# A two-stage Fourier and mixer kernel: the set-up of batch 0 and its hand-over to the chunks put in another order

## The chip, the cores and the metric

The kernel runs on one core of a Trainium2 chip. A core has five engines that each work through their own list of instructions in order: TensorE (PE: matrix products; PEld is its weight load), VectorE (DVE), ScalarE (ACT), GpSimd (POOL) and SyncE (SP, which here only issues transfers). GpSimd and ScalarE issue transfers too. An instruction that waits for another engine's result holds up all that stands behind it on its own engine. The metric is the device time of one execution in microseconds.

## The reference, cut to what matters

```python
x: (8, 3136, 256)   U: (3136, 32)   V: (32, 3136)   w1: (256, 1024)   w2: (1024, 256)
X = fft(fft(x, axis=1), axis=2).real          # per batch: 3136 x 256
h = (X.transpose(0, 2, 1) @ U @ V).transpose(0, 2, 1)
u = X + h                                     # rank-32 mixing along the sequence
out = u + relu(u @ w1) @ w2                   # per row, 256 -> 1024 -> 256
```

## The kernel before, in words

**Tables.** The transform along the sequence is done as matrix products with tables of sines (`tabs[0]`) and cosines (`tabs[1]`) that the kernel makes at the start. A table has eight rows i of two halves each, 393 columns wide, and behind these 32 columns that hold U, already transformed. Rows with even i are made whole (`odd_row`); of the rows 7, 5, 3, 1 only the upper half is computed (`phase` on VectorE, a Sin on ScalarE, line 226), and `mirror_even` (line 325) writes the lower half as a mirrored copy, over `turned_copy` (line 318): on GpSimd when the sign is plus (rows 5 and 1 of the sines), on ScalarE when it is minus. The cosine rows are copies of sine rows (`cosine_odd`, `cosine_low`, `cosine_high`) or made by Abs and Sin (lines 232 and 233).

**Input of batch 0.** x of one batch arrives in two halves a = 0, 1, forward (`xf`) and reversed (`xr`). `along_d` (line 360, VectorE) folds the 256 channels into 128 sums and 128 differences (`EOF_`, `EOR_`), `alone` (line 366, GpSimd) copies the lone channel. For batch 0 one half of the fold along the sequence is done on TensorE, as products with an identity or a flip matrix (`fold_pe`, line 756), and evicted to `G` by ScalarE (`evict_g`); the other half on VectorE (`mirror`, `half`, lines 369 and 373). `load_second(a)` loads batch 1's half a into the same `xf` and `xr`; it issues one plain and one indirect transfer from GpSimd's queue and two small ones from SP's. `g_zeros` and `va_zeros` clear the unused parts of `G` and `VA` on GpSimd.

**U.** `transform_u(typ)` gives four steps for the sine table (`us`) and four for the cosine table (`uc`): `contract` (16 products, line 286), `keep` (a copy on ScalarE, line 292), `turn` (8 products, line 299), `evict` (two copies on ScalarE into the table's last 32 columns, lines 304 and 305).

**Sequence products.** `seq(b, par, typ, pn)` (line 411) multiplies `G` with a table, four products each. The call with pn = 0 leaves a copy `ev` on ScalarE, the call with pn = 1 gives on VectorE: a 32-column sum into `TAB` (line 433), an "up" sum (440) and a "down" sum (444) into `A` (typ 1) or `B` (typ 0). The wide result covers 128 channels; the lone channel, one row, is done by `narrow` (line 488), called by `first_channel` for batches 0 and 1 and by `column_steps` for the six others together: 16 products of 32 columns, one copy `evc`, and in `sums(par)` a sum into the row of `VA` (509), a 32-element sum `tc` (515) and, with par = 1, the sum of both `tc` (517). `finish` casts it into `low` (556).

**Hand-over.** `lowrank(0)` (line 599) multiplies `low` and `TAB` to give the low-rank operand `TA`. `chan` (line 562) makes from `A` and `B` the transformed rows `S` (h = 0, copied by ScalarE) and `T` (h = 1, for batch 0 copied by VectorE), in pieces of columns cut at 0, 393, 512, 785, 1177, 1569. `front(c)` (line 627) forms `u` of chunk c, 512 rows: a product of `TA` and `VA` (634), to which VectorE adds `S` and `T` (642), then a transposing transfer on SP's queue (645).

**Chunks.** There are 49 chunks. Each has eight steps j; in a step, `first_product` (two products of 512 columns, line 654, and a Relu on ScalarE, 656), on odd j `second_product` of the chunk before (eight products of 256 columns, line 670, three sums on VectorE, 676 to 679, and the store), then what the dictionary `due` holds for step 8c + j, and at j = 3 the `front` of the next chunk. `spread` puts the fold of batch 1 into steps 4 to 23 and its transform behind that; `column_loads` go to SP's queue from step 8.

**What sets the order.** Up to the end of chunk 0 the order is the one written (`tc.manual_schedule()`, closed at c = 1); after that a planner orders the instructions, except those that `pin` holds. Semaphores between the engines are put in by the framework, from the tiles and the address ranges that two instructions touch. Tiles of one tag share their buffers, so a new one waits until an old one is released: three PSUM buffers for tag "dft", three for "p1", two for "p2", two SBUF buffers for "ev".

Of the kernel before, what the change touches and what calls it, by code (L numbers as in the profile page):

```python
# [27 lines left out]
def kernel(  # L28
# [296 lines left out]
    def mirror_even(t, i):  # L325

        odd_m = (i + 1) // 2 % 2 == 1
        turned_copy(cells(t, i, 0, 1, NH - 1, 1), cells(t, i, NQ - 1, -1, NH - 1, 0),
                    1 if odd_m == (t == 0) else -1)

# [156 lines left out]

    def narrow(nb, stationary, dst, tc_, tag=("dft", 3), late=None):

        t = {}  # L490

        def products():
            pt = t["pt"] = psum.tile([P, QW], FP32, tag=tag[0], name="ptc", bufs=tag[1])
            for n in range(NI // 2):
                for g in range(4):
                    pn, par = divmod(g, 2)
                    i = ktiles(pn)[n]
                    nc.tensor.matmul(pt[g * R:(g + 1) * R], stationary(par, i),
                                     tabs[1][:kp(i), i, par, :],
                                     start=(n == 0), stop=(n == NI // 2 - 1))  # L500
            t["ev"] = wp.tile([P, QW], FP32, tag="ev", name="evc", bufs=2)
            nc.scalar.copy(t["ev"][2 * R:], t["pt"][:2 * R])
        yield products

        def sums(par):
            e, o = (t[k][(2 + par) * R:(2 + par) * R + nb] for k in ("ev", "pt"))
            up = dst[:, HALF // 2 - par:(0 if par else None):-2]
            dn = dst[:, HALF // 2 + 2 - par:HALF + 1 - par:2]
            nc.vector.tensor_tensor(up, o[:, par:NQ], e[:, par:NQ], op=AL.add)
            down = lambda: nc.vector.tensor_tensor(dn, e[:, 1:NQ], o[:, 1:NQ], op=AL.subtract)  # L510
            if late is None:
                down()
            else:
                late.append(down)
            nc.vector.tensor_tensor(tc_[:, par], o[:, NQ:QW], e[:, NQ:QW], op=AL.add)
            if par:
                nc.vector.tensor_tensor(tc_[:, 0], tc_[:, 0], tc_[:, 1], op=AL.add)
        for par in range(2):
            yield lambda par=par: sums(par)

    def column_steps():
# [18 lines left out]
        yield fold_c  # L540
        yield from narrow(NB, lambda par, i: GC[par][:kp(i), i * NB:i * NB + R], rows, tc_)

# [7 lines left out]
    def first_channel(b, **kw):  # L550
        tc_ = cpool.tile([1, 2, R], FP32, name=f"tc{b}", tag=f"tc{b}")
        dst = VA[b][R:R + 1]
        yield from narrow(1, lambda par, i: G[b][par][:kp(i), i, 256:256 + R], dst, tc_, **kw)

        def finish():
            nc.vector.tensor_copy(low[:1, b * R:(b + 1) * R], tc_[:, 0])
        yield finish
        mid = (HALF + S) // 2
        for lo, hi in ((HALF + 1, mid), (mid, S)):
            yield lambda lo=lo, hi=hi: nc.scalar.copy(dst[:, lo:hi], dst[:, S - lo:S - hi:-1])  # L560

    def chan(b, lo, hi, h, tag=("dft", 3)):
        d = ST[b]
# [4 lines left out]
                         start=False, stop=True)  # L568
        (nc.vector.tensor_copy if b == 0 and h == 1 else nc.scalar.copy)(
            d["ST"[h]][:, lo:hi], pt[:, :hi - lo])  # L570
# [27 lines left out]

    def lowrank(b):
        pt = psum.tile([P, 256], FP32, tag="dft", name="ptt", bufs=3)  # L600
        nc.tensor.matmul(pt[:], low[:, b * R:b * R + P], ones[:], start=True, stop=False)
        for n in range(4):
# [134 lines left out]
    mirror_even(0, 1)  # L737
    alone(0, xr, EOR_)
    alone(0, xf, EOF_)
    g_zeros(0)  # L740
    cosine_odd(4)
# [35 lines left out]
    for part in range(2):  # L777
        along_d(0, xf, EOF_, part)
    fold_pe(0, EOF_)

    def load_second(a):
        load_r(1, a)
        load_f(1, a)
        load_0(1, a, nc.sync)

    load_second(0)
    halve(1)
    mirror(0, slice(0, 128), AL.subtract)
    us[0]()
    us[1]()  # L790
    us[2]()
    busy(3, tabs[0])
# [21 lines left out]
    for par in range(2):  # L814
        half(0, par, slice(256, 258))
    load_second(1)
    evict_g(0)
# [3 lines left out]

    ta_rows(0)
    va_zeros(0)
    nc.gpsimd.memset(TAB[:, 4 * R:].bitcast(I32), 0)
# [10 lines left out]
    narrow_0 = list(first_channel(0, tag=("p2", 2), late=late))  # L835
    seq(0, 0, 0, 0)
    seq(0, 0, 0, 1)
    narrow_0[0]()
    seq(0, 1, 0, 0)
    for step in narrow_0[1:4]:  # L840
        step()
    late.insert(0, seq(0, 1, 0, 1))
    lowrank(0)
    cuts = (0, 393, 512, 785, 1177, HALF + 1)
    for n in range(2):
        for h in range(2):
            chan(0, cuts[n], cuts[n + 1], h, ("p2", 2) if n and h else ("p1", 3))
    tc.no_sync_barrier()
# [3 lines left out]
    for h in range(2):  # L852
        chan(0, cuts[2], cuts[3], h)
    for step in late:
# [7 lines left out]

    due = {n: [lambda n=n: chan(0, cuts[3 + n // 2], cuts[4 + n // 2], n % 2)] for n in range(4)}
    due.update({4: [lambda: last_row(0)], 5: narrow_0[4:5], 6: narrow_0[5:6], 44: [column_flips]})

# [61 lines left out]
```

## Time and profile before

| | us |
|---|---|
| median of 3 runs | 461.48 |
| lowest and highest | 458.42, 462.24 |
| the profiled execution | 462.04 |
| its span, first to last instruction | 459.0 |
| TensorE busy in the span | 443.2 (97%) |
| VectorE, ScalarE, GpSimd busy | 355.9, 296.2, 70.0 |
| mean granted TensorE clock | 0.996 |

Times in rows of the profile are counted from the start of the span. A row of the order of time has start, length, engine, line, operation, out<-in, shapes, the number of instructions, and in brackets the idle time before it with what ended it. Shares of busy time hide that the set-up (the first 40 us or so) and the chunks have different limits. Ends of TensorE's products are modelled, and spans on GpSimd are rough.

### The profile page before, as it was taken

What the parts mean: (1) busy time and instruction counts of PE and PEld (TensorE: products, weight loads), DVE (VectorE), ACT (ScalarE), POOL (GpSimd) and SP (SyncE); (2) the same over time, 40 slices, a digit from 0 to 9 for tenths busy, and PEclk for the clock granted to TensorE, in tenths of its full rate; (3) what the DMA queues carried; (4) which work ended last, traced back from release to release, by engine and by line L of the source; (5) the groups of instructions that cost most, each with busy time, mean ns of one, the idle gap of its engine ahead of it and who ended that gap; (6) DMA issues with size and microseconds to landing.
All of it is one profiled execution on the core that took longest, in us unless ns stands there. A gap on an engine that the chain in (4) does not pass through costs nothing.

```text
span 459.0 us, 8105 instructions
## 1 busy us (share of the span) xinstructions
PE 443.2 (97%) x2989; PEld 323.1 (70%) x3042; DVE 355.9 (78%) x818; ACT 296.2 (65%) x568; POOL 70.0 (15%) x112
## 2 busy tenths in 40 slices
PE   8878999999999999999999999999999999999996
PEld 6435766676777777777777777777777777777775
DVE  8997999878898769976997779967898666443433
ACT  7766645866965577665865577655865586655562
POOL 7980612100022002100102002200000000000000
PEclk9998999999999999999999999999999999999999
DMA  7995888995377826684298436792253323333343
GB/s 212 205 236 103 175 202 159 140 210 147 117 202 185 175 71 163 192 222 121 71 226 205 134 87 178 198 224 76 70 95 113 93 83 102 93 115 96 113 119 110
DMA packets 102955, 66.98 MB, mean 146 GB/s; under 512 B 73526, under 2 KB 99328, under 8 KB 99776
## 3 DMA queue, kind: packets, MB, share of 16 engines
q1 hardware_dynamic: 97762, 40.73, 38.6%
q0 software_dynamic: 5136, 25.74, 20.6%
q8 instruction: 23, 0.38, 0.3%
q14 instruction: 16, 0.13, 0.1%
q10 hardware_dynamic: 18, 0.00, 0.0%
HBM read 29.33 MB, written 25.69 MB: 120 GB/s over the span
## 4 chain that ended last, share of the span: by engine, by line
PE 83%; DVE 8%; issue 2%; DMA 2%; ACT 2%; POOL 1%; SPq 1%; DVEq 0%; POOLq 0%
PE p L670 34%; PE p L654 31%; PE pt L426 5%; PE ph L634 4%; PE pth L402 2%; DVE eor L360 2%; DVE eof L360 2%; DMA ut<-u 1%; PE pst L577 1%; PE pst L586 1%; DVE u L642 1%; DMA cr<-in_x_dram 1%; SPq L482 1%; PE ptt L603 1%; PE pg L761 1%
## 5 line engine op out<-in xcount | busy, mean ns | idle before, releaser
L656 ACT ACTIVATE h<-p 128x512 bf16<-128x512 f32 x392 | 223.6, 598 | 129.9 <-PE p L654 106.0
L654 PE MATMUL p<-u,w 128*128 128x512 bf16 x733 | 209.8, 379 | 2.6 <-ACT h L656 0.9
L670 PE MATMUL p<-w,h 128*128 128x256 bf16 x1568 | 204.0, 273 | 1.3
L670 PEld LDWEIGHTS <-h 128*128 128x128 bf16 x1568 | 153.1, 98 | 51.8 <-issue 0.6
L654 PEld LDWEIGHTS <-w 128*128 128x128 bf16 x784 | 106.0, 144 | 36.2 <-issue 3.0
L676 DVE TENSOR_TENSOR o<-p,ut 128x4 f32<-128x4 f32 (+1 forms) x100 | 16.5, 165 | 58.2 <-PE p L670 55.3
L55 POOL DMA_INDIRECT xf<-in_x_dram,xidx x16 | 20.3, 1269 | 184.7 <-DVE eof L360 172.6
L679 DVE TENSOR_TENSOR o<-p,ut 128x254 f32<-128x254 f32 (+1 forms) x100 | 40.9, 409 | 0.0
L678 DVE TENSOR_TENSOR o<-p,ut 128x254 f32<-128x254 f32 (+1 forms) x100 | 40.9, 409 | 0.0
L360 DVE TENSOR_TENSOR eor<-xr 99x1024 bf16<-99x1024 f32 x32 | 39.7, 1250 | 0.0
L360 DVE TENSOR_TENSOR eof<-xf 99x1024 bf16<-99x1024 f32 x32 | 39.0, 1236 | 0.0
L642 DVE TENSOR_TENSOR u<-ph,S 128x512 bf16<-128x512 f32 (+15 forms) x64 | 35.2, 559 | 0.0
L642 DVE TENSOR_TENSOR u<-ph,T 128x512 bf16<-128x512 f32 (+15 forms) x64 | 35.1, 559 | 0.0
L634 PE MATMUL ph<-va,ta 128*128 128x512 bf16 (+15 forms) x126 | 29.3, 329 | 0.1
L426 PEld LDWEIGHTS <-g 98*128 98x128 bf16 (+1 forms) x152 | 14.8, 98 | 13.6 <-issue 1.1
L369 DVE TENSOR_TENSOR eos<-eof,eor 99x1024 bf16<-99x1024 bf16 (+2 forms) x32 | 20.4, 654 | 0.0
L373 DVE TENSOR_TENSOR g<-eos 99x2048 bf16<-99x2048 bf16 (+3 forms) x18 | 18.6, 1048 | 0.2
L588 DVE TENSOR_TENSOR S<-evd,pst 128x392 bf16<-128x392 f32 (+1 forms) x24 | 13.6, 566 | 6.5 <-PE pst L586 6.1
L433 DVE TENSOR_TENSOR tab<-pt,ev 128x32 bf16<-128x32 f32 x32 | 6.1, 190 | 15.4 <-PE pt L426 14.3
L426 PE MATMUL pt<-tabs,g 98*128 98x425 bf16 x80 | 17.4, 344 | 0.0
L426 PE MATMUL pt<-tabc,g 98*128 98x425 bf16 x72 | 15.5, 343 | 0.6 <-ACT tabc L304 0.6
L73 POOL DMA_DIRECT2D xr<-in_x_dram x14 | 8.1, 575 | 40.5 <-DVE eor L360 40.2
(170 smaller groups left out, 361.6 us busy)
## 6 DMA issues: line engine op xcount, KB each, us to landing
out_dram<-o SPq DMA_DIRECT2D x48, 512.0 KB
xr<-in_x_dram POOLq DMA_DIRECT2D x14, 784.0 KB, 6.7
xr<-in_x_dram SPq DMA_DIRECT2D x2, 784.0 KB
ut<-u SPq DMA_TRANSPOSE x49
w<-in_moe_w_ch_dram POOLq DMA_DIRECT2D x1, 512.0 KB, 14.8
out_dram<-o SPq DMA_DIRECT2D x4, 128.0 KB
va<-in_moe_V_dram POOLq DMA_DIRECT2D x2, 196.0 KB, 5.0
xf<-in_x_dram,xidx POOLq DMA_INDIRECT x16, 7.3
```

What stands on the lines that cost most here:

```text
L55: nc.gpsimd.indirect_dma_start(out_, None, bass.AP(t.tensor, t.offset, [[w, rows], [1, w]]), bass.IndirectOffsetOnAxis(idx, 0), element_of ...
L360: pin(nc.vector.tensor_tensor(dst[:, a, :, part * P:(part + 1) * P].rearrange("p i (k t) -> p i k t", k=2), lo, hi, op=AL.subtract if part ...
L369: pin(nc.vector.tensor_tensor(EOS[:, a, :, cols], EOF_[:, a, :, cols], EOR_[:, a, ::-1][:, :, cols], op=op))
L373: pin(nc.vector.tensor_tensor(G[b % 2][par][:, :, cols], EOS[:, 0, :, cols], EOS[:, 1, :, cols], op=AL.add if par == 0 else AL.subtract))
L426: nc.tensor.matmul(pt[:], g[:kp(i), i, P * typ:P * (typ + 1)], tabs[typ][:kp(i), i, par, :], start=(n == 0), stop=(n == NI // 2 - 1))
L634: nc.tensor.matmul(ph[:, col:col + hi - lo], TA[b % 2][:k, s * P:(s + 1) * P], VA[b % 2][:k, lo:hi], start=True, stop=True)
L642: nc.vector.tensor_tensor(u[:, s, col:col + hi - lo], ph[:, col:col + hi - lo], src, op=AL.add)
L654: nc.tensor.matmul(p1[:], W1[:, s, j::JT], k["u"][:, s, :], start=(s == 0), stop=(s == 1))
L656: LAST[0] = nc.scalar.activation(k["h"][:, j, :], p1[:], AF.Relu)
L670: nc.tensor.matmul(p2[:, t % w, :], h[:, j, rs], W2[:, j, :], start=(j == 0), stop=(j == JT - 1))
L678: nc.vector.tensor_tensor(o[:, ts, 1:P], p2[:, :w, 1:P], ut[:, ts, 1:P], op=AL.add)
L679: nc.vector.tensor_tensor(o[:, ts, P + 1:D], p2[:, :w, P + 1:D], ut[:, tT, P - 1:0:-1], op=AL.add)
```

## The change

In the set-up of batch 0: the mirrored half of row 1 is a ScalarE copy instead of a GpSimd copy. The two `alone` copies of half 0 and `g_zeros(0)` go to places behind U's first steps in the written order; the identity products of half 0's forward part go behind U's first contraction; `load_second(1)` goes behind `ta_rows(0)`.

In `narrow`: each `tc` sum goes ahead of the row's sum, and the sum of both is written to a place that the caller names: for `first_channel` straight into `low` (`finish` with its cast goes), for `column_steps` into `tc` as before.

In the hand-over: the narrow products of batch 0 and their sums stand ahead of the four sine sequence calls; `lowrank(0)` issues eight products of `ones` into its PSUM tile first; the T copy of columns 393 to 512 is ScalarE's instead of VectorE's; batch 1's T copies are ScalarE's in both. The two pieces of columns 785 to 1177 go from steps 0 and 1 to steps 1 and 2, those of 1177 to 1569 from steps 2 and 3 to 8 and 9 (chunk 1), `last_row(0)` from 4 to 10, and the two ScalarE copies that complete the narrow row from 5 and 6 to 12 and 14.

```diff
     def mirror_even(t, i):
 
         odd_m = (i + 1) // 2 % 2 == 1
-        turned_copy(cells(t, i, 0, 1, NH - 1, 1), cells(t, i, NQ - 1, -1, NH - 1, 0),
-                    1 if odd_m == (t == 0) else -1)
+        dst, src = cells(t, i, 0, 1, NH - 1, 1), cells(t, i, NQ - 1, -1, NH - 1, 0)
+        if i == 1:
+            nc.scalar.copy(dst, src)
+        else:
+            turned_copy(dst, src, 1 if odd_m == (t == 0) else -1)
...
             up = dst[:, HALF // 2 - par:(0 if par else None):-2]
             dn = dst[:, HALF // 2 + 2 - par:HALF + 1 - par:2]
+            nc.vector.tensor_tensor(tc_[:, par], o[:, NQ:QW], e[:, NQ:QW], op=AL.add)
+            if par:
+                nc.vector.tensor_tensor(total, tc_[:, 0], tc_[:, 1], op=AL.add)
             nc.vector.tensor_tensor(up, o[:, par:NQ], e[:, par:NQ], op=AL.add)
...
-            nc.vector.tensor_tensor(tc_[:, par], o[:, NQ:QW], e[:, NQ:QW], op=AL.add)
-            if par:
-                nc.vector.tensor_tensor(tc_[:, 0], tc_[:, 0], tc_[:, 1], op=AL.add)
...
-        yield from narrow(1, lambda par, i: G[b][par][:kp(i), i, 256:256 + R], dst, tc_, **kw)
-
-        def finish():
-            nc.vector.tensor_copy(low[:1, b * R:(b + 1) * R], tc_[:, 0])
-        yield finish
+        yield from narrow(1, lambda par, i: G[b][par][:kp(i), i, 256:256 + R], dst, tc_,
+                          low[:1, b * R:(b + 1) * R], **kw)
...
-        (nc.vector.tensor_copy if b == 0 and h == 1 else nc.scalar.copy)(
+        (nc.vector.tensor_copy if dve else nc.scalar.copy)(
...
-    def lowrank(b):
+    def lowrank(b, fill=0):
         pt = psum.tile([P, 256], FP32, tag="dft", name="ptt", bufs=3)
+        for _ in range(fill):
+            nc.tensor.matmul(pt[:], ones[:, :P], ones[:], start=True, stop=True)
...
     cosine_low(1)
     mirror_even(0, 1)
-    alone(0, xr, EOR_)
-    alone(0, xf, EOF_)
-    g_zeros(0)
     cosine_odd(4)
     load_v()
...
-    fold_pe(0, EOF_)
...
+    alone(0, xr, EOR_)
+    alone(0, xf, EOF_)
     load_second(0)
+    g_zeros(0)
     halve(1)
     mirror(0, slice(0, 128), AL.subtract)
     us[0]()
     us[1]()
+    fold_pe(0, EOF_)
     us[2]()
...
-    load_second(1)
...
     ta_rows(0)
+    load_second(1)
     va_zeros(0)
...
     narrow_0 = list(first_channel(0, tag=("p2", 2), late=late))
-    seq(0, 0, 0, 0)
-    seq(0, 0, 0, 1)
-    narrow_0[0]()
-    seq(0, 1, 0, 0)
-    for step in narrow_0[1:4]:
+    for step in narrow_0[:3]:
         step()
-    late.insert(0, seq(0, 1, 0, 1))
-    lowrank(0)
+    for par in range(2):
+        for pn in range(2):
+            late.append(seq(0, par, 0, pn))
+    late = [late[-1]] + late[:2]
+    lowrank(0, 8)
     cuts = (0, 393, 512, 785, 1177, HALF + 1)
     for n in range(2):
         for h in range(2):
-            chan(0, cuts[n], cuts[n + 1], h, ("p2", 2) if n and h else ("p1", 3))
+            chan(0, cuts[n], cuts[n + 1], h, ("p2", 2) if n and h else ("p1", 3), h > n)
...
     for h in range(2):
-        chan(0, cuts[2], cuts[3], h)
+        chan(0, cuts[2], cuts[3], h, dve=h == 1)
...
-    due = {n: [lambda n=n: chan(0, cuts[3 + n // 2], cuts[4 + n // 2], n % 2)] for n in range(4)}
-    due.update({4: [lambda: last_row(0)], 5: narrow_0[4:5], 6: narrow_0[5:6], 44: [column_flips]})
+    def piece(n, h):
+        return [lambda: chan(0, cuts[n], cuts[n + 1], h, dve=h == 1)]
+
+    due = {1: piece(3, 0), 2: piece(3, 1), 8: piece(4, 0), 9: piece(4, 1), 10: [lambda: last_row(0)],
+           12: narrow_0[3:4], 14: narrow_0[4:5], 44: [column_flips]}
```

More of the change, by code (lines that the diff above doesn't have):

```diff
@@ L486, in column_loads, with narrow @@
                     yield load
-    def narrow(nb, stationary, dst, tc_, tag=("dft", 3), late=None):
+    def narrow(nb, stationary, dst, tc_, total, tag=("dft", 3), late=None):
         t = {}
@@ L540, in column_steps @@
         yield fold_c
-        yield from narrow(NB, lambda par, i: GC[par][:kp(i), i * NB:i * NB + R], rows, tc_)
+        yield from narrow(NB, lambda par, i: GC[par][:kp(i), i * NB:i * NB + R], rows, tc_,
+                          tc_[:, 0])
         def finish():
@@ L560, in first_channel, with chan @@
             yield lambda lo=lo, hi=hi: nc.scalar.copy(dst[:, lo:hi], dst[:, S - lo:S - hi:-1])
-    def chan(b, lo, hi, h, tag=("dft", 3)):
+    def chan(b, lo, hi, h, tag=("dft", 3), dve=False):
         d = ST[b]
```

## The prediction

> **What bounds the kernel now.** I read the page first, then the set-up in order of time, because the diff touches only what is issued before chunk 2, and last the stretches behind it, to see whether a lead survives there. The page's busy shares and slices:
>
> ```profile
> PE 443.2 (97%) x2989; PEld 323.1 (70%) x3042; DVE 355.9 (78%) x818; ACT 296.2 (65%) x568; POOL 70.0 (15%) x112
> ...
> PE   8878999999999999999999999999999999999996
> ...
> PEclk9998999999999999999999999999999999999999
> ```
>
> TensorE is 97% busy. Its gaps lie in the first four slices (11.5 us each), and so does the one dip of the granted clock. So the change can win or lose only in the first 46 us; the sum asks how much earlier the chunks start.
>
> The set-up in order of time (start, length, engine, line, operation):
>
> ```profile
> 10.66 0.53 ACT L323 ACTIVATE tabs<-tabs 99x392 bf16<-99x392 bf16 x1
> 13.21 0.60 ACT L232 ACTIVATE ab<-phe,c 99x394 f32<-99x394 int32 x1
> 14.68 1.51 POOL L321 COPY tabc<-tabs 99x394 bf16<-99x394 bf16 x1
> 14.93 0.58 ACT L773 CAST gu<-pf 99x512 bf16<-99x512 f32 x1
> 15.15 1.16 PE L166 MATMUL idle<-tabs 98*128 98x393 bf16 x6
> 16.25 1.38 POOL L321 COPY tabs<-tabs 99x392 bf16<-99x392 bf16 x1
> 17.19 0.67 DVE L310 TENSOR_SCALAR tabc<-tabc,hv 99x786 bf16<-99x786 bf16 x1
> 17.29 0.62 ACT L233 ACTIVATE tabc<-ab,c 99x394 bf16<-99x394 f32 x1
> 18.28 0.85 PE L286 MATMUL pu<-tabs,gu 98*32 98x393 bf16 x16
> 19.19 0.49 ACT L292 CAST wu<-pu 128x393 bf16<-128x393 f32 x1 [1.27 <-PE pu L286]
> 19.73 0.92 PE L299 MATMUL put<-sel,wu 128*98 128x64 bf16 x8 [0.59 <-ACT wu L292]
> 22.84 1.34 POOL L55 DMA_INDIRECT xf<-in_x_dram,xidx  x1 [0.30 <-issue]
> ```
>
> The chain runs from U's contraction (18.28) over its copy on ScalarE (19.19) and the turning product (19.73) to the same again for the cosine table, and then to the sequence products:
>
> ```profile
> 26.86 0.17 DVE L373 TENSOR_TENSOR g<-eos 99x16 bf16<-99x16 bf16 x1
> 28.04 1.60 PE L426 MATMUL pt<-tabs,g 98*128 98x425 bf16 x8
> 29.09 0.75 POOL L183 MEMSET va<- 1x785 int32 x1
> 29.58 0.91 PE L498 MATMUL ptc<-tabc,g 98*32 98x425 bf16 x16
> 29.86 0.59 DVE L440 TENSOR_TENSOR B<-pt,ev 128x393 bf16<-128x393 f32 x1
> 30.35 0.58 DVE L444 TENSOR_TENSOR B<-pt,ev 128x392 bf16<-128x392 f32 x1
> 30.42 1.62 PE L426 MATMUL pt<-tabs,g 98*128 98x425 bf16 x8
> 30.54 0.51 ACT L502 COPY evc<-ptc 64x425 f32<-64x425 f32 x1 [1.06 <-PE ptc L498]
> 31.15 0.58 DVE L509 TENSOR_TENSOR va<-ptc,evc 1x393 bf16<-1x393 f32 x1 [0.21 <-POOL mc L833]
> 31.39 0.52 ACT L430 COPY ev<-pt 128x425 f32<-128x425 f32 x1 [0.35 <-PE pt L426]
> 32.76 0.18 DVE L517 TENSOR_TENSOR tc<-tc 1x32 f32<-1x32 f32 x1
> 33.04 1.44 DVE L556 CAST low<-tc 1x32 bf16<-1x32 f32 x1
> 33.05 1.40 POOL L182 MEMSET va<- 32x1568 int32 x1
> 34.51 0.19 DVE L433 TENSOR_TENSOR tab<-pt,ev 128x32 bf16<-128x32 f32 x1
> 34.54 0.40 PE L601 MATMUL ptt<-ones,low 128*128 128x256 bf16 x1 [2.50 <-DVE low L556]
> ```
>
> TensorE stands 2.50 us for a cast of 32 elements that takes 1.44 us, as long as the GpSimd memset beside it, and the last `tab` sum queues behind that cast. What the gap does to the clock (busy time of PE, PEld, DVE, ACT, POOL in each microsecond, then the granted clock), and how the first `u` follows:
>
> ```profile
> 34.00:35.00 1.00, 0.46 (x3) 0.28 (x4) 0.97 (x3) 0.00 (x0) 0.95 (x2) 0.51 0.97 164
> 35.00:36.00 1.00, 1.00 (x6) 0.63 (x5) 0.19 (x1) 0.11 (x1) 0.60 (x3) 0.50 0.76 123
> 37.00:38.00 1.00, 1.00 (x9) 0.73 (x8) 0.85 (x3) 0.26 (x1) 0.00 (x0) 0.79 0.57 139
> ...
> 37.15 0.76 DVE L569 CAST T<-pst 128x393 bf16<-128x393 f32 x2 [1.95 <-PE pst L567]
> 38.45 0.68 DVE L642 TENSOR_TENSOR u<-ph,T 128x512 bf16<-128x512 f32 x1
> 42.69 0.57 DVE L569 CAST T<-pst 128x392 bf16<-128x392 f32 x1 [0.86 <-PE pst L567]
> ```
>
> The clock is at half from the end of the gap until about 37.4, some 3 us. Behind that:
>
> ```profile
> 47.00:55.00 8.00, 7.81 (x54) 5.71 (x54) 8.00 (x13) 5.59 (x12) 4.57 (x6) 1.00 0.66 159
> 55.00:63.00 8.00, 7.38 (x50) 5.10 (x48) 8.00 (x16) 3.98 (x8) 4.51 (x5) 1.00 1.10 233
> ...
> 61.38 0.44 PE L654 MATMUL p<-u,w 128*128 128x512 bf16 x1 [0.35 <-DVE u L642]
> ```
>
> From 47 to 63 us VectorE never stops and TensorE waits for its `u`. So the lead that lasts is VectorE's.
>
> **The change, part by part.** Times are on the clock of the profile before.
>
> *1. Mirror of sine row 1 from GpSimd to ScalarE.* GpSimd loses 1.38 us. ScalarE gets 0.53 us (the like copy at 10.66), ahead of the operation at 13.21. In the built program this copy waits for GpSimd's copy out of the same row, which ends at 14.68 + 1.51 = 16.19. ScalarE takes its instructions in order, so it stands from 13.3 to 16.2 and copies until 16.8. Queued behind it is everything from 13.21 to the end of the 17.29 row, 4.70 us, which now ends at 21.5. The `gu` copy moves from 15.51 to 19.1; U's contraction needs it, and starts at 19.1 (before 18.28). The copy at 19.19 now starts at 21.5 and the turning product at 22.0: **+2.3 us** for TensorE and all that follows on it. The ends: if the wait were already met, ScalarE would carry only 0.53 us more, the 19.19 copy would start at 18.45, and this would be -0.7; if nothing overlapped it would be 2.9 + 0.53 = +3.4. I take +2.3, since the rows give both ends of the wait.
>
> That contraction now stands ahead of the identity products (`fold_pe`), which slide into TensorE's new gap between 20.0 and 22.0: nothing, instead of the 0.7 above. VectorE's halving (17.19) waits for the same ScalarE queue and moves by 1.4; its last fold (26.86 + 0.17) then ends by 28.5, ahead of the narrow products at 28.04 + 2.3 = 30.3: nothing.
>
> GpSimd's moves: `alone` and the zeros of G go behind the loads of batch 1, half 0, one of which (22.84) ends at 24.2 in the old order and earlier in the new, with 1.38 us less before it. The G evictions that now wait for those zeros run after 25. The loads of half 1 go ahead of the zeros of VA: these ended at 29.84, the loads wait for a VectorE row that is up to 1.4 late, so 31.3; the first narrow row is written at about 31.9. Cover 0.6 us; without it, up to 1 us. SP issues the same list in the same order.
>
> *2. The clock in the new gap.* TensorE has nothing between 15.15 + 1.16 = 16.3 and 19.1: 2.8 us. The gap of 2.50 us ended at half clock for about 3 us. Then the contraction takes 1.7 for 0.85, and four products of 512 columns take 1.7, for 256 columns take 0.109 at full clock:
>
> ```profile
> 107.34 0.87 PE p L670 x8
> ```
>
> They end at 19.1 + 1.7 + 1.7 = 22.5 and the turning product waits 0.5: **+0.5**. Ends: 0, and +3.0 if all products up to the sequence products run at half clock. [...]
>
> *3. Narrow products first, `low` written by the last sum.* Leaving out the shift of 1 and 2, the narrow products take the slot at 28.04, end at 28.95, and `evc` is there at 29.5. On VectorE: two `tc` sums, the sum into `low` (0.18 each, from 32.76) and two `va` sums (0.58), 1.8 with gaps, to 31.3; a `tab` sum and two B sums (29.86 and 30.35 show 0.5 from start to start), to 32.5. The last `ev` copy has to wait for the buffer which the second B sum frees: 0.52, to 33.1. The last `tab` ends at 33.3 (before 34.70). TensorE has finished at 28.04 + 0.91 + 1.60 + 1.62 = 32.2; the eight filling products need a PSUM buffer that the same B sum frees, and run 8 x 0.109 from 32.5 to 33.4. So the low-rank product starts at 33.4, not 34.54: **-1.1**. Ends: -2.4 (TensorE alone) and 0.
>
> [...]
>
> *4. Warm clock.* The gap of TensorE shrinks to about 0.3. From 34.54 it has five products of 256 columns and 2048 columns of `chan`, 1.4 us at 0.109 per 256, twice that at half clock: at most -1.4. ScalarE's copies in between do not shorten, so I take -1.0, and -0.2 for the 119-column T copy that leaves VectorE ahead of `u` (the pair at 37.15 takes 0.76, one wide copy 0.57): **-1.2**. Ends 0 and -1.6.
>
> *5. Late pieces to chunk 1.* VectorE's wait of 0.86 us for the piece at 42.69 falls away: **-0.86**. The piece's copy and `last_row` are done some 3 us later by the same busy VectorE and are not saved. ScalarE's copies of the narrow row follow into 47 to 55, where it has 2.4 us to spare. Ends 0 and -0.86. Past chunk 1 a planner sets the order: batch 1 loses one VectorE copy, about 0, within 0.4 either way.
>
> Sum: 2.3 + 0.5 - 1.1 - 1.2 - 0.86 = -0.4 us. The profiled execution took 462.04 (span 459.0 and 3.0 around it), 0.56 above the median 461.48, so 461.6 there and **461.1** as a median.
>
> **The rivals.**
> A. *The wait in 1 is met early.* Part 1 gives -0.7 and 2 nothing: -0.7 - 1.1 - 1.2 - 0.86 = -3.9, 457.6. For it: GpSimd's recorded spans are rough. Against: its copies stand there back to back, the next one starts at 16.25.
> B. *Slower: the clock stays low.* The 2.8 us gap at 16.3 keeps the clock at half until the sequence products, +3.0 for +0.5: +2.1, 463.6. It is slower than before as soon as part 2 costs over 0.9. For it: gaps in the products go on after 19.1. Against: at 34.5 three busy microseconds were enough.
> C. *It doesn't do what it says.* The new wait stays, TensorE's later gap still halves the clock, and VectorE finds another wait in chunk 0: 4 and 5 give nothing, 2.3 + 0.5 - 1.1 = +1.7, 463.2. Against: the fills stand right in that gap.
>
> **How the numbers follow.** Forecast 0.62, with 459.8 to 462.6 from the halves of its bounds; A 0.14; B 0.14; C 0.10. The range reaches from A to beyond B and C with part 3 short by 1.1: 457.5 to 464.8. One per cent, about what a measurement of this kernel can tell from no change, is 4.6 us. Below 456.9 lies only more than A: 0.07. Above 466.1 lies B with the later gains missing as well: 0.09. Within: 0.84.
>
> **What would show it.** Part 1: ScalarE idle from 13.3 to 16.2, released by GpSimd, and the turning product at about 22. Part 2: clock near 0.5 between 19 and 22.5. Part 3: a `low` sum of 0.2 us, the fills running until the last `tab`. Part 4: clock 1.0 from there to the first `u`, which ends near 39.6 (before 39.13). Part 5: no wait of VectorE before the second `u`, and the first `o` about 0.4 earlier than before. The forecast is wrong if ScalarE does not stand, or if the clock falls for longer than 3 us.

## The result, and the profile after

| | before | after |
|---|---|---|
| median of 20 executions | 461.80 us | 464.81 us |
| lowest, highest | 458.42, 467.85 | 461.06, 470.49 |
| first profiled execution | 462.04 | 461.43 |

The ratio after to before is 1.0064 [1.0039, 1.0088]: 3.0 us slower, 3.7 us above the forecast of 461.1 and just past the end of the range (464.8). Yet the profiled execution is 0.61 us faster than that of before, where the working had -0.4. Both are true, because the executions of the changed kernel fall into two groups by the mean clock that each lists: five at 0.992 to 0.993 with a median of 461.43, and fifteen at 0.985 or less with one of 465.11. The first profile is of the first kind; a second profile, taken in the experiments, is of the second. Some executions also lose time in a wait of TensorE between 100 and 105 us, far behind the change (4.16 us in one profile, whose row stands under "Both gaps filled", 3.52 us in another). A ratio is taken over the executions within 1.5% of the fastest of their kernel, so it leaves out part of the long ones.

The first profile after, page (span and slices):

```profile
span 459.7 us, 8169 instructions
...
PEclk9889999999999999999999999999999999999999
```

Before, the dip of the clock lay in the fourth slice; now it lies in the second and third. The same execution in order of time; for comparison, first the first `u` and the first `o` of before:

```profile
37.84 0.69 DVE L642 TENSOR_TENSOR u<-ph,S 128x512 bf16<-128x512 f32 x1
50.82 0.16 DVE L676 TENSOR_TENSOR o<-p,ut 128x4 f32<-128x4 f32 x1
```

```profile
14.68 0.52 POOL L321 COPY tabc<-tabs 99x394 bf16<-99x394 bf16 x1
...
15.23 0.52 ACT L330 COPY tabs<-tabs 99x392 bf16<-99x392 bf16 x1 [1.94 <-POOL tabc L321]
18.02 0.97 PE L286 MATMUL pu<-tabs,gu 98*32 98x393 bf16 x16 [1.72 <-ACT gu L773]
...
20.81 0.94 PE L299 MATMUL put<-sel,wu 128*98 128x64 bf16 x8
24.38 1.36 PE L286 MATMUL pu<-tabc,gu 98*32 98x393 bf16 x16
33.61 0.18 DVE L514 TENSOR_TENSOR low<-tc 1x32 bf16<-1x32 f32 x1
35.63 1.05 PE L603 MATMUL ptt<-ones 128*128 128x256 bf16 x8 [0.70 <-DVE B L447]
36.51 0.27 PE L604 MATMUL ptt<-ones,low 128*128 128x256 bf16 x1
38.41 0.69 DVE L645 TENSOR_TENSOR u<-ph,S 128x512 bf16<-128x512 f32 x1
39.02 0.68 DVE L645 TENSOR_TENSOR u<-ph,T 128x512 bf16<-128x512 f32 x1
...
50.42 0.17 DVE L679 TENSOR_TENSOR o<-p,ut 128x4 f32<-128x4 f32 x1
```

ScalarE stands for GpSimd's copy, as forecast, and TensorE stands 1.72 us for ScalarE's `gu`; the turning product comes at 20.81 and the second contraction at 24.38 (before 19.73 and 21.96). The copy into `low` is gone, the fills run until the low-rank product, the first `u` ends at 39.70 (before 39.13), and the first `o` starts 0.40 earlier than at 50.82.

The clock of this execution, by stretches set to the edges of its dip (columns as in the prediction's windows: busy time of PE, PEld, DVE, ACT, POOL, then the granted clock):

```profile
11.81:15.22 3.41, 3.38 (x17) 2.23 (x16) 2.63 (x5) 1.46 (x3) 3.35 (x4) 1.00 1.03 250
15.22:18.63 3.41, 1.70 (x23) 0.74 (x21) 3.38 (x4) 3.33 (x7) 3.41 (x6) 1.00 1.01 214
18.63:22.05 3.42, 3.42 (x22) 1.70 (x15) 3.39 (x6) 3.36 (x8) 2.99 (x5) 0.50 1.08 202
22.05:25.46 3.41, 3.41 (x23) 1.28 (x20) 3.27 (x5) 0.75 (x2) 2.35 (x7) 0.50 1.05 237
```

Half clock for 6.8 us, behind a stretch in which TensorE was busy 1.70 of 3.41 us. A mean clock of 0.992 says the same for the whole span: 2 x 0.008 x 459.7 = 7.4 us at half. By that sum the 0.985 of most executions is 13.9 us. The sum doesn't say where in the span the dips lie.

### The profile page after: what moved, and what is told of

It is laid out like the page before. It is cut to its first block, busy times and chain, and to the rows that moved or that the text cites. A ratio compares the mean times of both kernels' runs of the same rounds, so it can differ in the third digit from the quotient of the medians.

```text
span 459.7 us, 8169 instructions
## 1 busy us (share of the span) xinstructions
PE 447.6 (97%) x3050; PEld 323.5 (70%) x3050; DVE 353.2 (77%) x815; ACT 296.4 (64%) x570; POOL 65.9 (14%) x111
## 4 chain that ended last, share of the span: by engine, by line
PE 88%; DVE 5%; ACT 3%; POOL 1%; issue 1%; DVEq 0%; ACTq 0%; POOLq 0%
PE p L673 35%; PE p L657 34%; PE pt L429 5%; PE ph L637 4%; PE pth L405 2%; PE pg L761 1%; ACT h L659 1%; PE pst L587 1%; PE pst L578 1%; PE ptt L606 1%; DVE eor L363 1%; DVE u L645 1%; DVE va L515 1%; POOL xf L55 1%; DVE eof L363 0%
## 5 line engine op out<-in xcount | busy, mean ns | idle before, releaser
L657 PE MATMUL p<-u,w 128*128 128x512 bf16 x784 | 219.0, 379 | 0.8 <-DVE u L645 0.7
L637 PE MATMUL ph<-va,ta 128*128 128x512 bf16 (+19 forms) x128 | 29.6, 329 | 0.0
```

The costliest lines, as they stand in the source:

```text
L637: nc.tensor.matmul(ph[:, col:col + hi - lo], TA[b % 2][:k, s * P:(s + 1) * P], VA[b % 2][:k, lo:hi], start=True, stop=True)
L657: nc.tensor.matmul(p1[:], W1[:, s, j::JT], k["u"][:, s, :], start=(s == 0), stop=(s == 1))
```

## The experiments

Theory after the result: ScalarE's wait opens the gap on TensorE (part 1), the gap puts TensorE at half clock, for 6.8 us in some executions and for twice that in most (part 2, with rival B's size), and the later parts give what they should. Rivals: the moved narrow products, the fills or the late pieces cost the 3 us; or the slow executions lose their time in the chunks. Executions with a mean clock under 0.99 and the medians, for all kernels run (the later batches' 77 executions of before; for the first 20 no clock is listed). An execution at 0.99 or more is called undisturbed below:

| kernel | executions | of them under 0.99 | median | median of the others |
|---|---|---|---|---|
| before | 77 | 32 | 462.04 | 461.03 |
| after | 20 | 15 | 464.81 | 461.43 |
| before, with the mirror on ScalarE | 12 | 10 | 465.95 | 461.85 |
| after, mirror on GpSimd again | 6 | 0 | 458.52 | 458.52 |
| after, first gap filled | 12 | 2 | 458.92 | 458.51 |
| after, mirror issued first (two batches) | 10 | 4 | 458.50 | 457.90 |
| ... without low-rank fills | 6 | 1 | 458.02 | 457.84 |
| ... late pieces in chunk 0 | 10 | 4 | 463.50 | 459.86 |
| ... with the cast | 4 | 1 | 459.89 | 458.24 |
| ... both gaps filled (two batches) | 16 | 0 | 457.87 | 457.87 |
| before, low-rank gap filled | 10 | 2 | 459.68 | 459.42 |
| before, both gaps filled (two batches) | 16 | 0 | 459.96 | 459.96 |
| after, both gaps filled | 12 | 0 | 460.56 | 460.56 |

### The mirror back on GpSimd

```diff
-        if i == 1:
-            nc.scalar.copy(dst, src)
-        else:
-            turned_copy(dst, src, 1 if odd_m == (t == 0) else -1)
+        turned_copy(dst, src, 1 if odd_m == (t == 0) else -1)
```

> The changed kernel with the mirror of sine row 1 back on GpSimd, all else as changed. Theory (the wait of ScalarE opens a gap of TensorE at 16.3 us, and in most executions the clock stays at half for about 14 us after it, not the 7 of the profiled one): no wait and no long gap, clock 0.996 or more, and the later gains of 3.2 us stay, 458 to 459.5 us, 0.6% under the kernel before. Rival (the later parts, the pieces in chunk 1 and the eight filling products, cost the 3 us): no faster than the changed kernel, 464 to 465.

Ratio to before 0.9899 [0.985, 0.9948], clock 1.0. In order of time:

```profile
15.26 1.38 POOL L321 COPY tabs<-tabs 99x392 bf16<-99x392 bf16 x1
16.70 0.85 PE L286 MATMUL pu<-tabs,gu 98*32 98x393 bf16 x16 [0.39 <-POOL tabs L321]
...
35.76 0.69 DVE L642 TENSOR_TENSOR u<-ph,S 128x512 bf16<-128x512 f32 x1
```

The gap ahead of the contraction shrinks from 1.72 to 0.39 us, and the first `u` starts at 35.76, 2.08 ahead of before's 37.84. So all the other parts together gain, and the 3 us come in only with the mirror on ScalarE. The time is in the 458 to 459.5 expected.

### That edit alone, in the kernel before

```diff
     def mirror_even(t, i):
...
-        turned_copy(cells(t, i, 0, 1, NH - 1, 1), cells(t, i, NQ - 1, -1, NH - 1, 0),
-                    1 if odd_m == (t == 0) else -1)
+        dst, src = cells(t, i, 0, 1, NH - 1, 1), cells(t, i, NQ - 1, -1, NH - 1, 0)
+        if i == 1:
+            nc.scalar.copy(dst, src)
+        else:
+            turned_copy(dst, src, 1 if odd_m == (t == 0) else -1)
```

> The kernel before with that one edit of the mirror alone. Theory: it waits as the changed kernel does, the clock falls at 18 us and once more in the old gap at 32 to 34.5 us, clock 0.985 or less, 465 to 469 us. Rival: within 1 us of the kernel before.

Ratio 1.005 [1.0012, 1.0089]; ten of twelve executions have a clock under 0.99. The profiled one, in stretches as above:

```profile
14.79:18.20 3.41, 1.53 (x9) 0.77 (x8) 1.94 (x2) 2.90 (x6) 2.49 (x6) 1.00 0.95 219
18.20:35.27 17.07, 15.37 (x76) 6.88 (x76) 10.43 (x19) 9.04 (x21) 10.42 (x17) 0.50 0.99 219
```

Half clock for 17.07 us. The edit alone makes the kernel slower. Taken by themselves the other parts gave -2.3 us (458.52 against 460.85, the median of the undisturbed executions of before in that batch); with the long dip there they give only 1.2 (from 466.32 here to 465.11 in the changed kernel, executions under 0.99). In the profiles with a long dip (here and in the changed kernel below) the low-rank stage behind it runs at a clock of 1.0, so that the second dip which was expected here is missing, and there is none for the fills to save; that this makes the difference was not tested. But the row ahead of TensorE's gap here is not ScalarE's:

```profile
16.26 2.36 DVE L363 TENSOR_TENSOR eof<-xf 99x1024 bf16<-99x1024 f32 x2 [1.81 <-DMA xf<-in_x_dram,xidx]
18.68 1.86 PE L764 MATMUL pg<-eof,flip 99*99 99x512 bf16 x4 [2.36 <-DVE eof L363]
```

In this order the column products stand ahead of U's contraction, and they wait for VectorE, which waits for the columns from memory, 1.81 us late here. There is a second cause of a gap at the same place, and it differs from execution to execution. The later runs take it up.

### The gap filled, the wait left in

```diff
-    busy(6, tabs[0])
+    busy(17, tabs[0])
```

> The changed kernel with 17 products without use instead of 6 ahead of U's contraction, so that TensorE is busy from 15.2 to 18.1 us; the wait of ScalarE stays. Theory: clock 0.995 or more, the wait itself costs only the 1.1 us by which U's copy comes later (20.3 for 19.2), 459.5 to 460.5 us. If the wait costs by itself and not through the clock: 464 to 465 with a clock near 1.

Ratio 0.9918 [0.988, 0.9955]; two of twelve executions under 0.99. The profiled one (465.83 us, 0.991) has a clock of 1.0 in the whole set-up; its dip of 6.8 us starts at 104.5, behind a wait of TensorE of 3.52 us. In order of time:

```profile
15.15 3.00 PE L166 MATMUL idle<-tabs 98*128 98x393 bf16 x17
18.08 0.85 PE L286 MATMUL pu<-tabs,gu 98*32 98x393 bf16 x16
...
36.59 0.69 DVE L645 TENSOR_TENSOR u<-ph,S 128x512 bf16<-128x512 f32 x1
```

ScalarE's rows are late as before, U's contraction starts at the same time as in the changed kernel (18.02), and nothing is computed sooner; only the clock stays at 1.0. The first `u` starts at 36.59 for 38.41: 1.82 us is the price of the 6.8 us at half clock, and 36.59 - 35.76 = 0.83 us that of the wait itself (1.1 was expected, and 459.5 to 460.5 us in all).

### The mirror issued ahead of GpSimd's copy

```diff
-    cosine_low(1)
     mirror_even(0, 1)
+    cosine_low(1)
```

> The changed kernel with the calls for the mirror of row 1 and the cosine copy of row 1 exchanged: the mirror stays on ScalarE and waits for nothing on GpSimd. Theory: U's copy starts near 18.5 instead of 20.3, no gap over 1 us, 457 to 458.5 us, faster than both. Rival: 464 to 465.

> The changed kernel with the row-1 sine mirror issued ahead of GpSimd's cosine copy, a second time, for its share of executions with the clock at half on the same chip as the kernel with both gaps filled. Theory: 458.2 us in executions with the clock at 1.0, and 463 or more with a clock of 0.985 in about a quarter (6 of the 22 executions of this head so far).

First batch: ratio 0.9887 [0.9824, 0.995]; second: 0.9941 [0.9885, 0.9996]. In order of time (first batch):

```profile
13.33 0.52 ACT L330 COPY tabs<-tabs 99x392 bf16<-99x392 bf16 x1
16.24 0.85 PE L286 MATMUL pu<-tabs,gu 98*32 98x393 bf16 x16
35.63 0.69 DVE L645 TENSOR_TENSOR u<-ph,S 128x512 bf16<-128x512 f32 x1
```

ScalarE's copy reads the same row as GpSimd's; issued first, it waits for nothing, and the 457.6 us of rival A come about (457.90 in the undisturbed executions). But four of ten executions have a clock under 0.99. The second batch's profile is of one:

```profile
16.06 2.37 DVE L363 TENSOR_TENSOR eof<-xf 99x1024 bf16<-99x1024 f32 x2 [1.62 <-DMA xf<-in_x_dram,xidx]
18.48 1.03 PE L761 MATMUL pg<-eof,flip 99*99 99x512 bf16 x4 [1.38 <-DVE eof L363]
22.25 1.23 DVE L363 TENSOR_TENSOR eof<-xf 99x1024 bf16<-99x1024 f32 x1 [2.29 <-DMA xf<-in_x_dram,xidx]
23.53 1.01 PE L761 MATMUL pg<-eof,flip 99*99 99x512 bf16 x2 [2.85 <-DVE eof L363]
```

No wait of ScalarE, but columns late by 1.62 and 2.29 us, gaps of 1.38 and 2.85 us, and half clock from 21.6 to 35.3.

### The changed kernel once more

> The changed kernel again, unchanged, for the profile of another execution. Theory (ScalarE's wait opens a gap of 1.7 us on TensorE, and the granted clock then stays at half for about 7 us in some executions and about 14 us in most): if the profiled execution is one near 464 us, its clock is at 0.5 from about 18 to about 32 us, the narrow products and their sums come about 3 us later than in the first profile, and from the first tab on every row is later by the same 3 us. If it is one near 461.5, its trace is that of the first profile. Rival (the executions near 464 lose their time in the main loop): the clock at half for 7 us only, and 3 us lost after 40 us.

This profile took 468.44 us (clock 0.980). Order of time, then stretches set to its dip:

```profile
15.59 2.62 DVE L363 TENSOR_TENSOR eof<-xf 99x1024 bf16<-99x1024 f32 x2 [1.14 <-DMA xf<-in_x_dram]
18.04 0.85 PE L286 MATMUL pu<-tabs,gu 98*32 98x393 bf16 x16 [1.72 <-ACT gu L773]
...
42.15 0.69 DVE L645 TENSOR_TENSOR u<-ph,S 128x512 bf16<-128x512 f32 x1
54.16 0.17 DVE L679 TENSOR_TENSOR o<-p,ut 128x4 f32<-128x4 f32 x1
```

```profile
14.13:17.54 3.41, 2.19 (x11) 0.95 (x9) 2.27 (x6) 2.23 (x5) 3.41 (x6) 1.00 0.96 224
17.54:20.96 3.42, 1.99 (x22) 0.88 (x22) 3.35 (x6) 3.39 (x7) 3.03 (x6) 1.00 1.09 184
20.96:24.37 3.41, 3.41 (x15) 1.74 (x15) 2.87 (x3) 1.83 (x5) 2.78 (x4) 0.50 1.06 237
24.37:27.78 3.41, 3.41 (x24) 1.52 (x24) 3.05 (x8) 1.56 (x3) 2.32 (x6) 0.50 0.92 225
27.78:31.20 3.42, 2.79 (x15) 1.46 (x14) 0.00 (x0) 2.22 (x6) 2.16 (x4) 0.50 0.99 223
31.20:34.61 3.41, 3.41 (x11) 1.32 (x9) 1.17 (x3) 1.64 (x6) 0.00 (x0) 0.50 0.95 211
```

The gap is the same 1.72 us as in the first profile, but here the clock falls at 20.96 and not at 18.63, and by stretches of the same length counted back from there the gap is parted between two of them. The first, busy 2.19 of 3.41 us, changes nothing; behind the second (1.99) the clock is at half for 13.65 us, and the sequence products run in it. The first `u` starts 3.74 later than in the first profile, the first `o` too. The theory's 3 us are there ahead of 40 us. The rest of this execution's loss lies behind: its rows fall back by another 4.0 us between 98 and 116 us, and the clock is low once more there: 0.96 between 100 and 140 us, by which about 3.2 us are at half. No profile shows one of the changed kernel's executions near 465 us; that they have the long dip without that second loss is an inference from their mean clock and from the 3.74 us here.

### Parts 3 to 5 one by one

On the kernel with the mirror issued first, each of the first three undoes one thing; the fourth is on the kernel before.

```diff
-    lowrank(0, 8)
+    lowrank(0)
```

> The changed kernel with the row-1 sine mirror issued ahead of GpSimd's cosine copy (458.5 us), and without the eight filling products of the low-rank stage. They lie in TensorE's wait for the narrow result; without them that gap of about 0.9 us becomes one of about 1.6 us. Theory (a gap of 1.7 us is enough to halve the clock): the clock falls near 35 us in some executions at least, 459.5 to 462 us in those. Rival (what halved the clock at 18 us was that TensorE had also been only partly busy before): nothing falls, 458.3 us.

Ratio 0.9885 [0.9788, 0.9982], undisturbed 457.84 against 457.90 with the fills. The gap that was expected to grow to 1.6 us is 0.71 in the profile, at a clock of 1.0:

```profile
36.62 0.28 PE L604 MATMUL ptt<-ones,low 128*128 128x256 bf16 x1 [0.71 <-DVE B L447]
```

One of six executions, 460.3 us at 0.995, may have a stretch of 3.4 us at half clock there; no profile shows it, and executions at 0.995 or 0.996 come with the fills too (464.32, 464.86 and 461.54 us in the next two runs). So no run shows that the fills still gain anything with the new order ahead of them.

```diff
-    due = {1: piece(3, 0), 2: piece(3, 1), 8: piece(4, 0), 9: piece(4, 1), 10: [lambda: last_row(0)],
-           12: narrow_0[3:4], 14: narrow_0[4:5], 44: [column_flips]}
+    due = {0: piece(3, 0), 1: piece(3, 1), 2: piece(4, 0), 3: piece(4, 1), 4: [lambda: last_row(0)],
+           5: narrow_0[3:4], 6: narrow_0[4:5], 44: [column_flips]}
```

> The changed kernel with the row-1 sine mirror issued ahead of GpSimd's cosine copy (458.5 us), the twelve late pieces, the last row and the va copies back among chunk 0's steps. By the prediction's last step (the pieces cost 0.86 us there, in front of the second u) it is 459.4 us, and the second u stands 0.85 us later than with the pieces in chunk 1. Rival (chunk 1's steps pay the same later): 458.5 us, with the u of the last chunks where they were.

Ratio 0.9975 [0.992, 1.0031]. The first `o` starts 12.98 behind the first `u`, as before (50.82 - 37.84), for 12.01 in the changed kernel, with the wait back that the prediction named:

```profile
40.91 0.69 DVE L645 TENSOR_TENSOR u<-ph,S 128x512 bf16<-128x512 f32 x1
45.76 0.57 DVE L570 CAST T<-pst 128x392 bf16<-128x392 f32 x1 [0.86 <-PE pst L568]
53.89 0.16 DVE L679 TENSOR_TENSOR o<-p,ut 128x4 f32<-128x4 f32 x1
```

The part is worth 0.97 us at the first `o`; the four executions with a clock of 0.998 or more took 458.95 to 460.61, against 457.63 to 458.71 in six with the pieces in chunk 1.

```diff
-                          low[:1, b * R:(b + 1) * R], **kw)
+                          tc_[:, 0], **kw)
+
+        def finish():
+            nc.vector.tensor_copy(low[:1, b * R:(b + 1) * R], tc_[:, 0])
+        yield finish
...
-    for step in narrow_0[:3]:
+    for step in narrow_0[:4]:
```

> The changed kernel with the row-1 sine mirror first, and the low-rank operand cast by an instruction of its own again, behind the second of the va copies. By the prediction's third step the cast cost 1.1 us where it lay beside a GpSimd memset of 1.4 us; with the narrow products first, it lies beside short memsets. Theory: in executions with the clock at 1.0, 458.4 us (the cast at its own 0.2); if it still meets the long memset, 459.5 us.

The interval, 0.9973 [0.9911, 1.0035], tells nothing; the rows do. The cast takes 0.20 us in its new place (1.44 beside the memset, before), and the two executions with a clock of 0.998 or more took 457.79 and 458.24, for 457.90 without it. As far as these two tell, what part 3 gained came from the order, not from the cast left out.

```profile
18.57 1.03 PE L765 MATMUL pg<-eof,flip 99*99 99x512 bf16 x4 [1.47 <-DVE eof L363]
31.85 0.20 DVE L561 CAST low<-tc 1x32 bf16<-1x32 f32 x1
```

The first of these rows is a gap of 1.47 us for late columns behind which this execution's clock stayed at 1.0.

```diff
-    def lowrank(b):
+    def lowrank(b, fill=0):
...
+        for _ in range(fill):
+            nc.tensor.matmul(pt[:], ones[:, :P], ones[:], start=True, stop=True)
...
-    lowrank(0)
+    lowrank(0, 24)
```

> The kernel before with 24 filling products in the low-rank stage, where it has none, so that its own gap of TensorE of 2.5 us ahead of the low product is covered. By the prediction's fourth step (the half clock from 34.5 to 37.4 us costs about 1.2 us with the sum it delays): the clock stays at 1.0 and the kernel takes 460.4 us. Rival (that stretch is VectorE's, and TensorE's clock there costs nothing): 461.5 us. Second rival (more filling products end later than the narrow result comes and delay the low product): 462 us.

Ratio 0.9951 [0.9897, 1.0006], which alone doesn't settle it; seven of ten executions at a clock of 1.0, 459.19 to 459.98, where before has most of its undisturbed executions at 0.995 or 0.996 and a median of 461.03. So half clock in the low-rank stage costs about 1.6 us (461.03 - 459.42); the prediction's -1.2 for part 4 was fair. The profiled execution has another dip, in the part that it shares with the kernel before, and no ScalarE wait in it:

```profile
18.06 1.03 PE L763 MATMUL pg<-eof,flip 99*99 99x512 bf16 x4 [1.74 <-DVE eof L360]
```

```profile
17.13:20.55 3.42, 1.89 (x21) 0.77 (x21) 3.39 (x6) 1.39 (x4) 3.42 (x7) 1.00 0.90 178
20.55:23.96 3.41, 3.41 (x15) 1.80 (x15) 3.41 (x4) 1.89 (x5) 3.02 (x4) 0.50 1.04 204
```

That is what the 32 of 77 executions of before under 0.99 look like, as far as this one stands for them.

### Both gaps filled

On the kernel with the mirror issued first:

```diff
     us[1]()
+    busy(6, tabs[0])
     fold_pe(0, EOF_)
     us[2]()
-    busy(3, tabs[0])
+    busy(10, tabs[0])
```

> The changed kernel with the row-1 sine mirror issued ahead of GpSimd's cosine copy, and with more filling products where TensorE waits for the gathered columns: six of them (1.0 us) ahead of the first four column products and ten instead of three (1.7 us) behind the turning product. In the last profiles the half clock lasted 1, 2, 3, 4 or 5 times 3.41 us and followed in six of seven on a stretch of 3.41 us in which TensorE was busy for at most 0.58 of the time. Theory (such a stretch halves the clock, and where the column data are late by a microsecond it comes about without ScalarE's wait too): with both waits filled nearly no execution has a clock under 0.993 from the set-up; 458.5 to 459 us (the fills themselves cost up to 0.3). Rival (the half clock comes from something else than TensorE's idle time): a third of the executions at 463 us or more and a clock of 0.985, as with the mirror first alone.

> Mirror first and both waits filled, a second time with more executions. Theory (idle time of TensorE alone decides): at most one execution in ten with a clock under 0.99; median 458.1 us. Rival (something else as well): about a third, as with the mirror first and the waits open, and a median that moves with them.

On the kernel before, beside the low-rank fills:

```diff
-    busy(6, tabs[0])
+    busy(13, tabs[0])
```

> The kernel before with both of its waits filled: 13 filling products instead of six ahead of the first column products, and 24 in the low-rank stage. Theory: the kernel before, too, has executions near 465 us only because its TensorE waits for late columns at 16 to 18 us; with the fills they become rare, and the time is that of its undisturbed executions with the covered low-rank gap, 459.3 us. Rival: nearly half of the executions stay at 464 to 466 us, clock 0.985.

> The kernel before with both of its waits filled, a second time with more executions. Theory: at most one execution in ten with a clock under 0.99, median 459.6 us. Rival: about two fifths of the executions, as in the kernel before.

On the changed kernel, the wait left in, 17 fills ahead of the contraction and ten behind the turning product:

> The changed kernel, ScalarE's wait left in, with 17 filling products instead of six ahead of the contraction and ten instead of three behind the turning product. Theory: the wait alone costs 0.8 us against the mirror first; 459 us, and at most one execution in ten with a clock under 0.99 (with the first fill alone it was three in twelve; in the changed kernel 15 of 20). Rival: a quarter or more stay at 464 us and above.

None of 44 executions has a clock under 0.99. Ratios: mirror first 0.9948 [0.9913, 0.9984] and 0.9916 [0.9888, 0.9945]; before filled 0.9984 [0.9948, 1.002] and 0.9994 [0.9964, 1.0025]; changed kernel filled 0.9968 [0.9923, 1.0012]. Only the first of these kernels has its intervals wholly under 1. That one, second batch, in stretches:

```profile
14.00:24.00 10.00, 9.95 (x81) 5.41 (x79) 9.97 (x14) 7.57 (x16) 9.70 (x12) 1.00 0.99 201
24.00:34.00 10.00, 8.67 (x66) 4.86 (x65) 8.02 (x24) 6.35 (x15) 9.12 (x26) 1.00 0.99 231
```

The added products compute nothing that is used, so in these kernels it is TensorE's idle time that puts an execution at half clock in the set-up (0 of 44 with both gaps filled; 32 of 77 of before, 15 of 20 of the changed kernel and 4 of 10 with the mirror first), be it ScalarE's wait or late columns that makes it. Five of the 44 are at 464.66 us or more with a clock of 0.993 to 0.996; the profile of one (before filled, 465.14 us) has its loss far behind the set-up, with a wait of 4.16 us and a clock of 0.91 between 100 and 120 us, and at 5 of 44 such a loss seems too rare to make the changed kernel's fifteen of twenty:

```profile
104.71 2.03 PE L656 MATMUL p<-u,w 128*128 128x512 bf16 x4 [4.16 <-DVE u L644]
```

The filled kernel before took 459.67 and 460.16 us (medians of its two batches), where 459.3 and 459.6 were expected.

The changed kernel's wait does no harm to the clock once it is covered, but costs its own time; and there the ten fills end later than the columns are ready: the products behind them start at 23.24 instead of 22.08. That accounts for 1.16 of the 2.05 us between its 460.56 and the 458.51 with the first gap filled alone; the rest is open. The filled kernel with the mirror first is the best found: 457.87 us over 16 executions, by its two ratios 2.4 and 3.9 us under before, with 15 of the 16 between 457.68 and 459.39.

## Why the prediction was wrong

**What failed is step 2, "the clock in the new gap": +0.5, from "the gap of 2.50 us ended at half clock for about 3 us".** The dip lasts 6.8 us in the first profile (0.992; a quarter of the executions have 0.992 or 0.993) and costs 1.82 us there; in the second profile, of a further execution at a mean clock of 0.980, it lasts 13.65 us and costs 1.82 + 3.74 = 5.6 us, beyond the bound of +3.0, as it reaches through the sequence products to the narrow ones. It does so although the gap measured 1.72 us, not the 2.8 of the working. Rival B had the mechanism, at a chance of 0.14 and with too small a price. The error behind it is one of reading: the length of a dip was taken from the only one in one profiled execution. The three times that were known, 458.42 to 462.24, already spread by 3.8 us; they fit the groups of before at a clock of 1.0 (about 459) and of 0.995 or 0.996 (about 461), as a dip that comes and goes between executions would make them; their own clocks are not listed.

**Step 1** (+2.3): the wait is there, but ends at 15.20 and not at 16.19, because GpSimd's copy took 0.52 us and not 1.51; VectorE's sum beside it had not begun, for want of its columns. The turning product came at 20.81, not 22. The wait by itself measured 0.83 us at the first `u`: with the gap filled the turning product comes 1.97 us later than with the mirror on GpSimd (20.82 against 18.85), but there TensorE has another wait behind it, for the second columns, which takes up the rest and is not there with the gap filled:

```profile
21.26 0.60 PE L758 MATMUL pg<-eof,flip 99*99 99x512 bf16 x2 [1.08 <-DVE eof L360]
```

So the term was too large by about 1.5.

**Steps 3 and 4** (-1.1 and -1.2): -2.3 at the first `u`, measured -2.08 with the mirror on GpSimd. The parts inside are another matter: the new order gave it, by what the runs show, not the cast (the sum into `low` took the 0.18 us that it was put at, at 33.61, beside GpSimd memsets of 0.18 and 0.19 us; in the four profiles whose rows show both it lies ahead of the memset of 1.40), and the fills are not shown to matter behind it. **Step 5** (-0.86): 0.97 at the first `o`.

**The sum.** At the first `u` of the profiled execution the working gives +2.3 + 0.5 - 2.3 = +0.5, and +0.57 was measured: 0.83 + 1.82 - 2.08. It came out right by two errors of opposite sign, and the profiled execution was one of the lucky quarter. Most of what "would show it" held there, up to the first `o` 0.4 earlier; ScalarE's wait and the turning product came about 1 us sooner than said, and the sign that did not hold was the clock, at half until 25.5 instead of 22.5, longer than the 3 us given as the point where the forecast fails. The chances have a hole, too: 0.07, 0.09 and 0.84 add up to 1, but say nothing of 464.8 to 466.1 us, where the median of 464.81 lies.

Rival A's price held (457.6; the mirror issued first takes 457.90 undisturbed), its event did not come. Rival C fell: in both profiles of the changed kernel the low-rank stage runs at a clock of 1.0, and part 5 gives what was said.

## What to carry to other kernels

When a move makes an engine wait (here ScalarE, 1.94 us), look at what TensorE does meanwhile: 1.7 us without work cost 0.8 us here as a wait and up to 5.6 us as a clock. Products whose result nobody reads, put into such a gap, were cheap insurance against a wait that varies: with both gaps filled none of 44 executions had a clock under 0.99. They have to end before the data come; ten that ended late cost 1.16 us. And a dip in one profiled execution is one draw: set the mean clock of every timed execution beside it before pricing it, and if the times spread by as much as the change is worth, the spread is what has to be explained.

## What the runs showed of the hardware

**Half clock came in whole multiples of 3.41 us.** Read in stretches of 0.2 us, the dips in the set-up lasted 3.41 us (before), 6.83 and 13.65 (the two profiles of the changed kernel), 17.07 (the mirror edit alone), 10.24 (without fills; pieces in chunk 0) and 13.65 (mirror first, second batch; before with the low-rank gap filled): 1, 2, 4, 5, 3, 3, 4 and 4 times 3.41. In the other nine profiles the clock stayed at 1.0 from 14 to 42 us. Further back, five profiles have a mean clock of 0.91 from 100 to 140 us (first gap filled; without fills; pieces in chunk 0), 0.91 from 100 to 120 (before, both gaps filled, second batch) and 0.96 from 100 to 140 (the changed kernel's second): by these shares about 7.2, 7.2, 7.2, 3.6 and 3.2 us at half, an estimate.

TensorE was busy for 0.43 to 0.58 of the last 3.41 us ahead of six of the eight falls in the set-up, and for 0.65 and 0.72 ahead of the other two; none of the eight stretches was wholly idle. Six other stretches of that length, counted off from the edges of dips, were busy for 0.62 to 0.71 and passed without a fall (two of before from 16.93 and 44.24; the mirror edit alone from 38.68; the changed kernel's second profile from 14.13; without fills from 34.27; pieces in chunk 0 from 16.21). Idle time as recorded is thus not all that counts. What ends a dip stays open: two wholly busy stretches were enough in the first profile (18.63 to 25.46), and were not in the second (20.96 to 27.78).

**Late columns.** VectorE's wait for the first gathered half of x is nothing in three profiles (before; without fills; mirror first with both gaps filled, second batch) and 0.19 to 1.81 us in ten others; for the second half it went up to 2.29. Why, was not tried.

**A GpSimd copy of 99x394 elements** took 1.51 to 1.56 us in four profiles (before; mirror first, first batch; without fills; mirror first with both gaps filled, second batch), in which VectorE had begun its two-input sum before it (14.38 to 14.63), and 0.52 in eight in which the sum began later (14.82 to 16.26), for want of its columns. Which of the two it is shifted the end of ScalarE's wait by a microsecond (15.20 for 16.19).
